# A gated linear attention and two feed-forward layers: the forward products of the gate are made by inverting the backward ones, not by a second scan

## The chip, the cores and the metric

The kernel runs on one core of one Trainium2 chip. The metric is the device time of one execution in microseconds (us). TensorE is the matrix engine (PE in the profile, PEld for its weight loads), VectorE is DVE, ScalarE is ACT, SyncE issues most DMAs (SP).

## The reference, cut to what matters

```python
def _attn_ref(q, k, v, alpha):
    B, H, S, D = q.shape                      # 4, 8, 768, 48
    state = np.zeros((B, H, D, D), dtype=np.float32)
    for t in range(S):
        state = alpha[:, :, t, :, None] * state + np.einsum('bhd,bhe->bhde', k[:, :, t], v[:, :, t])
        y[:, :, t] = np.einsum('bhd,bhde->bhe', q[:, :, t], state)
    return y

x = attention output as rows of 384           # 3072 tokens
g = leaky_relu(x @ w_in, 0.01);  x = g @ w_out     # 384 -> 2048 -> 384
g = elu(x @ w_in2);              out = g @ w_out2  # 384 -> 2048 -> 384
```

`alpha` is between 0.8 and 1.0 and acts per head dimension and token. The attention is made in 24 units of 128 tokens (a chunk of all 8 heads of one batch element).

## The kernel before, in words

For a unit u the host lays out `seqs[u]`: alpha, k and q, all with the head dimension on the partitions (112 rows, two heads with a gap between them) and four groups of 128 tokens along the row. Alpha has one extra column in front of each group (129 columns a group, 517 in all with the last), so that a scan over the whole row starts afresh at each group. One DMA brings all of it into a tile `pack` (three buffers).

`prep_k(u)` (L124 to L135) makes, on VectorE: a scan E from the right over alpha (L129), the product of all later alphas of the chunk; `pe` (L131), the product of the whole chunk, clamped; its reciprocal into the four start columns of the constant tile `d1` (L132); and k times E, in place in `pack` (L134). `prep_F(u)` (L137 to L142) is a second scan F from the left over alpha (L141), which starts at 1/pe and so gives the reciprocal of E at each token. `prep_q(u)` (L144) multiplies q by F in place (L146). Then TensorE makes the scores `sc` of k and q (L160) and transposes k into `pk` (L168); ScalarE copies that into `kn` (L175); VectorE masks the scores into `A` (L182) and decays the state, `T` = S times pe (L189); TensorE makes the output `po` (L214, L220) and the state's update `pu` (L233); VectorE adds up the state S (L257).

The feed-forward layers split each float32 operand into a high and a low part in the format fp32r and use three matmuls for one. For each of 16 slices of 128 hidden units: `hp` (L306), its activation `t` (ScalarE L312, then VectorE's max, L317), the high part `gh` (ScalarE L321), the low part `gl` (VectorE L327), and the sums `y` (L350). There are two buffers of `hp`, and two each of `gh` and `gl`. The weights are converted on the way by `convert_p`, `convert_a`, `convert_b` (L276 to L291).

The order of the work has two parts. The head, units 0 to 7 in the functions `quarter` and the loop behind them (L686 to L783), is fixed: `in_order()` chains the instructions of each engine as they are written. In `quarter(u, 0)` stands `prep_k(u + 1)`, in `quarter(u, 2)` stand `prep_F(u + 1)` and `prep_q(u + 1)`, so unit 8 is prepared there too. From there on (L784 on), where the units 8 to 23 run between the slices of layer 1, a scheduler places the instructions by a model of its own; each engine then works its list in order. Layer 2 follows with no attention in it.

Of the kernel before, what the change touches and what calls it, by code (L numbers as in the profile page):

```python
# [8 lines left out]
F32 = mybir.dt.float32  # L9
# [4 lines left out]
ALU = mybir.AluOpType  # L14
# [5 lines left out]
def attention_two_layers_kernel(  # L20
# [12 lines left out]
    nc = tc.nc  # L33
# [4 lines left out]
    C = CHUNK  # L38
    NU = NT // C
    NC = SEQ // C  # L40
    NP = H // 2
    PD = 2 * D
    PR = 64 + D
    KD = DM // 128
    KF = DFF // 128
    EXT = NP * (C + 1) + 1

    const = ctx.enter_context(tc.tile_pool(name="const", bufs=1))
# [4 lines left out]
    gs_p = ctx.enter_context(tc.tile_pool(name="gs", bufs=2))  # L53
    pack_p = ctx.enter_context(tc.tile_pool(name="pack", bufs=3))
    v_p = ctx.enter_context(tc.tile_pool(name="v", bufs=3))
    pe_p = ctx.enter_context(tc.tile_pool(name="pe", bufs=3))
    at_p = ctx.enter_context(tc.tile_pool(name="at", bufs=1))
    ps_y = ctx.enter_context(tc.tile_pool(name="ps_y", bufs=1, space=PSUM))
    ps_h = ctx.enter_context(tc.tile_pool(name="ps_h", bufs=2, space=PSUM))
# [3 lines left out]
    causal = const.tile([128, C], F32, name="causal")  # L63
    minus = const.tile([PR, PR], F32R, name="minus")
    d0 = const.tile([PR, EXT], F32, name="d0")
    d1 = const.tile([PR, EXT], F32, name="d1")
    bias = const.tile([PR, 2], F32, name="bias")
    outside = const.tile([PR, NU], F32, name="outside")
    far_sum = const.tile([PR, 2], F32, name="far_sum")
# [15 lines left out]
    def constants():  # L85
        make_identity(nc, ident)
        nc.scalar.activation(minus, ident[0:PR, 0:PR], ACTF.Copy, scale=-1.0)
        nc.gpsimd.memset(causal, 1.0)
        nc.gpsimd.affine_select(
            out=causal, in_=causal, compare_op=ALU.is_ge, fill=0.0,  # L90
            base=0, pattern=[[1, C]], channel_multiplier=-1,
        )
        nc.vector.memset(d0, 0.0)
        nc.vector.memset(d0[:, 0:EXT:C + 1], 1.0)
        nc.vector.memset(d1, 0.0)
        nc.vector.memset(bias[:, 0:1], -1.0)
        nc.vector.memset(bias[:, 1:2], -ALPHA_SPAN)
        nc.vector.memset(far_sum[:, 1:2], 1.0)
# [4 lines left out]
    st = {}  # L103
# [17 lines left out]
    def ext(t, off):  # L121
        return t[:, off:off + NP * (C + 1)].rearrange("p (g c) -> p g c", c=C + 1)

    def prep_k(u):  # L124
        t = packs.pop(u)
        kS = t[:, EXT:EXT + NP * C].rearrange("p (g c) -> p g c", c=C)
        qh = t[:, EXT + NP * C:].rearrange("p (g c) -> p g c", c=C)
        E = at_p.tile([PR, EXT], F32, tag="E", name="E")
        nc.vector.tensor_tensor_scan(E[:, ::-1], t[:, EXT - 1::-1], d0[:, ::-1], 0.0, ALU.mult, ALU.add)  # L129
        pe = pe_p.tile([PR, NP, 1], F32, tag="pe", name="pe")  # L130
        nc.vector.tensor_scalar(pe, ext(E, 0)[:, :, 1:2], 1e24, 1e-24, ALU.min, ALU.max)  # L131
        nc.vector.reciprocal(ext(d1, 0)[:, :, 0:1], pe)  # L132
        e2 = E[:, 1:EXT].rearrange("p (g c) -> p g c", c=C + 1)
        nc.vector.tensor_mul(kS, kS, e2[:, :, 1:C + 1])  # L134
        st[u] = dict(kS=kS, qh=qh, pe=pe, pack=t)  # L135

    def prep_F(u):  # L137
        d = st[u]
        t = d["pack"]
        F = at_p.tile([PR, EXT], F32, tag="F", name="F")  # L140
        nc.vector.tensor_tensor_scan(F[:, 0:EXT - 1], t[:, 0:EXT - 1], d1[:, 0:EXT - 1], 0.0, ALU.mult, ALU.add)  # L141
        d["F"] = F  # L142

    def prep_q(u):  # L144
        d = st[u]
        nc.vector.tensor_mul(d["qh"], d["qh"], ext(d.pop("F"), 0)[:, :, 1:C + 1])  # L146

    def attn_prep(u):
        prep_k(u)
        prep_F(u)  # L150
        prep_q(u)
# [352 lines left out]
    def conv_args(layer, kind, m):  # L504
# [10 lines left out]
        else:  # L515
            tags = (("cT", "S"), ("E", "F"))[n]
            tp, ts = [at_p.tile([128, 384], I32, tag=g, name=f"c{g}") for g in tags]
# [152 lines left out]
    with ExitStack():  # L670
        load_unit(0, True)
        constants()
        load_unit(1)
        load_v(0)
# [11 lines left out]
        def quarter(u, i, chain=True):  # L686
            j = unit_block[u]
            xh, xl, _, t = xtile(j)
            off = (u - blocks[j][0]) * C
            if i == 0:  # L690
                attn_pu(u)
                prep_k(u + 1)
                attn_T(u)
            elif i == 1:
                attn_mask(u)
                if chain:
                    attn_pk(u + 1)
                    attn_kn(u + 1)
                attn_po(u)
            elif i == 2:  # L700
                prep_F(u + 1)
                attn_state(u)
                prep_q(u + 1)
                if chain:
                    attn_sc(u + 1)
                attn_xh(u, xh, off)
                attn_rest(u, xh, off)
                load_unit(u + 3)
                load_v(u + 3)
            else:  # L710
                attn_xl_act(u, xl, off)
                st.pop(u)
                if u == blocks[j][0] + blocks[j][1] - 1:
                    gather(t, blocks[j][1] * C)
# [48 lines left out]
        for s, e in enumerate(seq):  # L763
# [3 lines left out]
            if s <= KF:  # L767
                c = 4 if s == 0 else 1 + FIRST + s - 2 - (s - 2) // 4 if s > 1 and s % 4 != 1 else 0
# [33 lines left out]
            if ph == 1 and j == NB - 1:  # L802
                if m == 0:
                    t = x2t[NT // 512 - 1].rearrange("p c f -> p (c f)").bitcast(I32)
# [13 lines left out]
            if ph == 2 and m >= KF - 10 and m % 2 == 0:  # L818
                u = 5 * j + (m - KF + 10) // 2
# [93 lines left out]
```

## Time and profile before

| what | value |
|---|---|
| runs: median (lowest to highest) of 3 | 961.44 us (958.7 to 961.64) |
| the profiled execution: its time, its span | 960.84 us, 959.1 us |
| busy: PE, DVE, ACT | 921.9, 530.0, 449.9 us |
| granted TensorE clock, mean | 0.982 of full speed |

The span is the time from the first to the last instruction, the profiled execution's own time has 1.7 us around it. A digit in the page's slices is the busy share of a fortieth of the span (24 us) in tenths. In the timeline a row is one instruction or a run of like ones, with its start, its duration and, in brackets, how long its engine sat idle before it and what released it. In the chain of waits a piece runs to the start of the next piece, so it can be shorter than the instruction.

### The profile page before, as it was taken

Reading aid. Unit: us, or ns where it says so; the run is one execution under the profiler, and the core shown is the slowest. Engines: PE = TensorE matmul, PEld = TensorE weight load, DVE = VectorE, ACT = ScalarE, POOL = GpSimd, SP = SyncE. Lnnn points to the kernel's source line nnn. Section 1 sums busy time; section 2 is a strip of 40 time slices with the busy share of each in tenths; the row PEclk is TensorE's granted clock in tenths of the full one; section 3 lists DMA queues with packets and bytes.
Section 4 is the critical chain, followed back from the end, with each engine's and each line's share of the span. In section 5 each row is a group of like instructions: output and inputs, shape, how many; then the busy total and the mean of one; then the engine's idle time right before and its main releaser. Section 6 shows DMA issues by size and latency. Waiting matters only on the chain.

```text
span 959.1 us, 13157 instructions
## 1 busy us (share of the span) xinstructions
PE 921.9 (96%) x5242; PEld 777.6 (81%) x5242; DVE 530.0 (55%) x872; ACT 449.9 (47%) x794; POOL 1.1 (0%) x8
## 2 busy tenths in 40 slices
PE   5687999999999999999999999999999999999997
PEld 4565776787888788788888889999999999899996
DVE  6876888855655547454479983433433433333332
ACT  1432765322322322323468894564654744744442
POOL 0000000000000000000000000000000000000000
PEclk9688999999999999999999999999999999999999
DMA  9737343222112121211224420010100200100001
GB/s 229 199 84 206 99 133 98 63 63 58 42 42 74 31 78 43 58 42 51 90 78 131 134 80 10 25 58 1 63 20 1 72 10 1 63 1 1 33 1 37
DMA packets 25092, 62.37 MB, mean 65 GB/s; under 512 B 3936, under 2 KB 7008, under 8 KB 25024
## 3 DMA queue, kind: packets, MB, share of 16 engines
q1 hardware_dynamic: 21360, 48.43, 17.9%
q10 hardware_dynamic: 3664, 13.04, 4.8%
q8 instruction: 43, 0.70, 0.3%
q14 instruction: 25, 0.20, 0.1%
HBM read 54.37 MB, written 4.72 MB: 62 GB/s over the span
## 4 chain that ended last, share of the span: by engine, by line
PE 83%; DVE 6%; DMA 4%; ACT 4%; issue 1%; SPq 1%; DVEq 0%; ACTq 0%
PE hp L381 21%; PE y L350 17%; PE hp L306 17%; PE oa L412 11%; PE o L412 11%; DMA pack<-in_seqs_dram 3%; PE po L214 2%; PE sc L160 2%; PE po L220 2%; DVE x2t L285 1%; DVE x2t L287 1%; DVE E L129 1%; PE pu L233 1%; ACT w L288 1%; ACT x2t L279 1%
## 5 line engine op out<-in xcount | busy, mean ns | idle before, releaser
L306 PE MATMUL hp<-x,w 128*128 128x512 f32 x864 | 219.2, 397 | 7.5 <-DMA x<-x 6.6
L381 PE MATMUL hp<-x,w 128*128 128x512 f32 x864 | 215.4, 393 | 0.0
L306 PEld LDWEIGHTS hp<-x,w 128*128 128x128 f32 x864 | 163.3, 190 | 45.8 <-DMA x<-x 8.1
L381 PEld LDWEIGHTS hp<-x,w 128*128 128x128 f32 x864 | 160.7, 188 | 29.3
L350 PE MATMUL y<-gh,w 128*128 128x512 f32 x576 | 178.2, 398 | 2.1 <-DVE x2t L359 1.1
L390 DVE SCALAR_TENSOR_TENSOR t<-t,hp 128x512 f32<-128x512 f32 x96 | 65.9, 687 | 148.7 <-ACT t L389 148.7
L350 PEld LDWEIGHTS y<-gh,w 128*128 128x128 f32 x576 | 106.1, 189 | 26.1 <-ACT x2t L363 1.3
L312 ACT ACTIVATE t<-hp 128x512 f32<-128x512 f32 x96 | 57.0, 595 | 118.8 <-PE hp L306 118.8
L350 PE MATMUL y<-gl,w 128*128 128x512 f32 x288 | 109.4, 394 | 0.9 <-DVE gl L327 0.9
L321 ACT CAST gh<-t 128x512 fp32r<-128x512 f32 x96 | 59.4, 620 | 102.5 <-PE y L350 55.9
L388 ACT ACTIVATE t<-hp 128x512 f32<-128x512 f32 x96 | 57.3, 597 | 105.7 <-PE hp L381 105.5
L82 DVE TENSOR_TENSOR gl<-t,gh 128x512 fp32r<-128x512 f32 x96 | 66.5, 692 | 70.0 <-ACT gh L79 68.4
L317 DVE TENSOR_TENSOR t<-t,hp 128x512 f32<-128x512 f32 x96 | 65.4, 681 | 69.3 <-ACT t L312 69.1
L412 PE MATMUL oa<-w,gh 128*128 128x384 f32 x384 | 96.7, 337 | 0.0
L412 PE MATMUL o<-w,gh 128*128 128x384 f32 x384 | 94.6, 336 | 0.0
L327 DVE TENSOR_TENSOR gl<-t,gh 128x512 fp32r<-128x512 f32 x96 | 66.1, 689 | 48.7 <-ACT gh L321 46.5
L79 ACT CAST gh<-t 128x512 fp32r<-128x512 f32 x96 | 59.5, 620 | 64.7 <-PE oa L412 34.8
L412 PEld LDWEIGHTS o<-w,gh 128*128 128x128 f32 x384 | 70.6, 188 | 5.4
L412 PEld LDWEIGHTS oa<-w,gh 128*128 128x128 f32 x384 | 70.2, 188 | 2.9
L350 PEld LDWEIGHTS y<-gl,w 128*128 128x128 f32 x288 | 54.3, 189 | 14.3 <-DVE gl L327 2.6
L412 PE MATMUL oa<-w,gl 128*128 128x384 f32 x192 | 63.0, 337 | 0.0
L389 ACT ACTIVATE t<-t 128x512 f32<-128x512 f32 x96 | 60.6, 632 | 2.3
(96 smaller groups left out, 834.9 us busy)
## 6 DMA issues: line engine op xcount, KB each, us to landing
stg<-in_w_dram SPq DMA_DIRECT2D x28, 384.0 KB, 3.1
pack<-in_seqs_dram ACTq DMA_DIRECT2D x13, 674.2 KB, 5.1
x2t<-in_w_dram SPq DMA_DIRECT2D x20, 384.0 KB, 3.5
pack<-in_seqs_dram SPq DMA_DIRECT2D x10, 674.2 KB, 5.4
span<-in_seqs_dram SPq DMA_DIRECT2D x24, 226.2 KB, 2.6
x2t<-in_w_dram SPq DMA_DIRECT2D x32, 144.0 KB, 2.6
out_dram<-osb SPq DMA_DIRECT2D x24, 192.0 KB, 2.0
vt<-in_vals_dram ACTq DMA_DIRECT2D x13, 288.0 KB, 5.2
```

Of the source, the lines that this page charges most:

```text
L79: nc.scalar.copy(dst, src)
L82: (lo_engine or nc.vector).tensor_sub(lo, src, dst.bitcast(F32))
L306: nc.tensor.matmul(hp, lhsT=a[:, kk, :], rhs=x[:, kk, :n], start=(i == 0), stop=(i == 3 * KD - 1))
L317: nc.vector.tensor_max(t, t, hp)
L321: nc.scalar.copy(gh, steps[1, j, m][0])
L327: nc.vector.tensor_sub(gl, t, gh.bitcast(F32))
L350: nc.tensor.matmul(ytiles[j][c], lhsT=a[:, c * 128:(c + 1) * 128], rhs=x, start=(first and i == 0), stop=(last and i == 2),)
L381: nc.tensor.matmul(hp, lhsT=a[:, kk, :], rhs=x[:, kk, :], start=(i == 0), stop=(i == 3 * KD - 1))
L388: nc.scalar.activation(t, hp, ACTF.Relu, scale=-1.0)
L389: nc.scalar.activation(t, t, ACTF.Exp, scale=-1.0)
L390: nc.vector.scalar_tensor_tensor(out=t, in0=t, scalar=-1.0, in1=hp, op0=ALU.add, op1=ALU.max)
L412: nc.tensor.matmul(otiles[j][i], lhsT=a[:, i * 128:(i + 1) * 128], rhs=x, start=(m == 0 and n == 0), stop=(m == KF - 1 and n == 2),)
```

## The change

The second scan is gone. E is kept, its 128 columns a group are inverted in place by one RECIPROCAL instruction on VectorE after k has been multiplied, and q is multiplied by the result. The tile E takes turns between two buffers (those that E and F had). `pe` is no tile of its own any more: `attn_T` reads it from E's first column of each group, which the inversion leaves alone. The clamp is now in the scan (`max` with 1e-24 in place of `add`). The tile `d1`, its memset and the small reciprocal into it are gone.

```diff
-    pe_p = ctx.enter_context(tc.tile_pool(name="pe", bufs=3))
...
-    d1 = const.tile([PR, EXT], F32, name="d1")
...
-        nc.vector.memset(d0, 0.0)
+        nc.vector.memset(d0, 1e-24)
         nc.vector.memset(d0[:, 0:EXT:C + 1], 1.0)
-        nc.vector.memset(d1, 0.0)
...
     def prep_k(u):
         t = packs.pop(u)
-        kS = t[:, EXT:EXT + NP * C].rearrange("p (g c) -> p g c", c=C)
-        qh = t[:, EXT + NP * C:].rearrange("p (g c) -> p g c", c=C)
-        E = at_p.tile([PR, EXT], F32, tag="E", name="E")
-        nc.vector.tensor_tensor_scan(E[:, ::-1], t[:, EXT - 1::-1], d0[:, ::-1], 0.0, ALU.mult, ALU.add)
-        pe = pe_p.tile([PR, NP, 1], F32, tag="pe", name="pe")
-        nc.vector.tensor_scalar(pe, ext(E, 0)[:, :, 1:2], 1e24, 1e-24, ALU.min, ALU.max)
-        nc.vector.reciprocal(ext(d1, 0)[:, :, 0:1], pe)
-        e2 = E[:, 1:EXT].rearrange("p (g c) -> p g c", c=C + 1)
-        nc.vector.tensor_mul(kS, kS, e2[:, :, 1:C + 1])
-        st[u] = dict(kS=kS, qh=qh, pe=pe, pack=t)
+        al, kq = t if isinstance(t, tuple) else (t[:, 0:EXT], t[:, EXT:])
+        kS = kq[:, 0:NP * C].rearrange("p (g c) -> p g c", c=C)
+        qh = kq[:, NP * C:].rearrange("p (g c) -> p g c", c=C)
+        E = at_p.tile([PR, EXT], F32, tag="EF"[u % 2], name="E")
+        nc.vector.tensor_tensor_scan(E[:, ::-1], al[:, ::-1], d0[:, ::-1], 0.0, ALU.mult, ALU.max)
+        e2 = E[:, 1:EXT].rearrange("p (g c) -> p g c", c=C + 1)[:, :, 1:C + 1]
+        nc.vector.tensor_mul(kS, kS, e2)
+        st[u] = dict(kS=kS, qh=qh, pe=ext(E, 0)[:, :, 1:2], e2=e2)
 
     def prep_F(u):
-        d = st[u]
-        t = d["pack"]
-        F = at_p.tile([PR, EXT], F32, tag="F", name="F")
-        nc.vector.tensor_tensor_scan(F[:, 0:EXT - 1], t[:, 0:EXT - 1], d1[:, 0:EXT - 1], 0.0, ALU.mult, ALU.add)
-        d["F"] = F
+        e2 = st[u]["e2"]
+        nc.vector.reciprocal(e2, e2)
 
     def prep_q(u):
         d = st[u]
-        nc.vector.tensor_mul(d["qh"], d["qh"], ext(d.pop("F"), 0)[:, :, 1:C + 1])
+        nc.vector.tensor_mul(d["qh"], d["qh"], d.pop("e2"))
```

The change moves VectorE's list at three kinds of places. (In these lists a scan is written SCALAR_TENSOR_TENSOR, `pack` is k or q of the unit, and a line number of the changed kernel is 2 to 8 lower: L127 is the scan, L129 k times E, L134 the inversion, L138 q times its result.)

VectorE in the head, the preparation of unit 4 in `quarter(3, ...)`, before:

```order
L129 SCALAR_TENSOR_TENSOR E<-pack,d_97 112x517
L131 TENSOR_SCALAR pe<-E 112x4
L132 RECIPROCAL d_98<-pe 112x4
L134 TENSOR_TENSOR pack<-pack,E 112x512
L189 TENSOR_TENSOR T<-S,pe 112x192
L182 TENSOR_TENSOR A<-sc_383,causal 128x512
L182 TENSOR_TENSOR A<-sc_384,causal 128x512
L141 SCALAR_TENSOR_TENSOR F<-pack,d_98 112x516
L257 TENSOR_TENSOR S<-pu,T 112x192
L146 TENSOR_TENSOR pack<-pack,F 112x512
```

and in the change:

```order
L127 SCALAR_TENSOR_TENSOR E<-pack,d_94 112x517
L129 TENSOR_TENSOR pack<-pack,E 112x512
L181 TENSOR_TENSOR T<-S,E 112x192
L174 TENSOR_TENSOR A<-sc_362,causal 128x512
L174 TENSOR_TENSOR A<-sc_363,causal 128x512
L134 RECIPROCAL E<-E 112x4x128
L249 TENSOR_TENSOR S<-pu,T 112x192
L138 TENSOR_TENSOR pack<-pack,E 112x512
```

Nothing else moved in the head: two small instructions are gone between E and k, and the inversion stands where F stood.

VectorE where the fixed order ends, the units 9 and 10, before:

```order
L129 SCALAR_TENSOR_TENSOR E<-pack,d_97 112x517
L131 TENSOR_SCALAR pe<-E 112x4
L134 TENSOR_TENSOR pack<-pack,E 112x512
L132 RECIPROCAL d_98<-pe 112x4
L129 SCALAR_TENSOR_TENSOR E<-pack,d_97 112x517
L141 SCALAR_TENSOR_TENSOR F<-pack,d_98 112x516
L131 TENSOR_SCALAR pe<-E 112x4
L134 TENSOR_TENSOR pack<-pack,E 112x512
L146 TENSOR_TENSOR pack<-pack,F 112x512
L132 RECIPROCAL d_98<-pe 112x4
L317 TENSOR_TENSOR t<-t,hp 128x512
L141 SCALAR_TENSOR_TENSOR F<-pack,d_98 112x516
```

and in the change (x2 is two in a row):

```order
L127 SCALAR_TENSOR_TENSOR E<-pack,d_94 112x517 x2
L129 TENSOR_TENSOR pack<-pack,E 112x512 x2
L134 RECIPROCAL E<-E 112x4x128 x2
L309 TENSOR_TENSOR t<-t,hp 128x512 x2
L138 TENSOR_TENSOR pack<-pack,E 112x512
L249 TENSOR_TENSOR S<-pu,T 112x192
L234 TENSOR_TENSOR x<-po,x 112x4x128
L138 TENSOR_TENSOR pack<-pack,E 112x512
L319 TENSOR_TENSOR gl<-t,gh 128x512 x2
```

Both inversions now stand ahead of the first max of `t` (L309); before, one F stood ahead of it and one behind it.

VectorE in the part that the scheduler orders, unit 12, before:

```order
L129 SCALAR_TENSOR_TENSOR E<-pack,d_97 112x517
L317 TENSOR_TENSOR t<-t,hp 128x512
L131 TENSOR_SCALAR pe<-E 112x4
L134 TENSOR_TENSOR pack<-pack,E 112x512
L132 RECIPROCAL d_98<-pe 112x4
L141 SCALAR_TENSOR_TENSOR F<-pack,d_98 112x516
L327 TENSOR_TENSOR gl<-t,gh 128x512
```

and in the change:

```order
L127 SCALAR_TENSOR_TENSOR E<-pack,d_94 112x517
L129 TENSOR_TENSOR pack<-pack,E 112x512
L134 RECIPROCAL E<-E 112x4x128
L309 TENSOR_TENSOR t<-t,hp 128x512
L174 TENSOR_TENSOR A<-sc_1625,causal 128x512
L174 TENSOR_TENSOR A<-sc_1626,causal 128x512
L138 TENSOR_TENSOR pack<-pack,E 112x512
L319 TENSOR_TENSOR gl<-t,gh 128x512
```

The max of `t` now stands behind the inversion; before, it stood right behind E.

## Rows read from the trace of the kernel before

**Rows 1.** The page: busy time of PE, busy tenths of PE and DVE, TensorE's waits at L350.

```profile
PE 921.9 (96%) x5242; PEld 777.6 (81%) x5242; DVE 530.0 (55%) x872; ACT 449.9 (47%) x794; POOL 1.1 (0%) x8
...
PE   5687999999999999999999999999999999999997
...
DVE  6876888855655547454479983433433433333332
...
L350 PE MATMUL y<-gh,w 128*128 128x512 f32 x576 | 178.2, 398 | 2.1 <-DVE x2t L359 1.1
```

**Rows 2.** Groups of DVE instructions: line, operation, tiles, shapes, count | busy us, mean ns.

```profile
L129 DVE TENSOR_TENSOR_SCAN E<-pack,d 112x517 f32<-112x517 f32 x24 | 29.6, 1233 | 24.7 <-DMA pack<-in_seqs_dram 24.7
L141 DVE TENSOR_TENSOR_SCAN F<-pack,d 112x516 f32<-112x516 f32 x24 | 29.4, 1225 | 0.1
L146 DVE TENSOR_TENSOR pack<-pack,F 112x512 f32<-112x512 f32 x24 | 16.5, 689 | 0.4
...
L291 DVE TENSOR_TENSOR w<-x2t,w 128x768 fp32r<-128x768 f32 x16 | 15.3, 958 | 5.1 <-ACT w L288 5.0
...
L284 DVE TENSOR_SCALAR x2t<-x2t 128x768 int32<-128x768 int32 x16 | 8.9, 554 | 0.0
...
L132 DVE RECIPROCAL d<-pe 112x4 f32<-112x4 f32 x24 | 4.2, 176 | 0.3
L131 DVE TENSOR_SCALAR pe<-E 112x4 f32<-112x4 f32 x24 | 4.1, 169 | 0.8
```

**Rows 3.** The instructions on the tile pe: durations in ns, least/median/most.

```profile
L131 DVE TENSOR_SCALAR pe<-E x24: 146/170/172, 5.8 to 422.3; 112x4 f32<-112x4 f32 x24
```

**Rows 4.** Timeline, 0 to 60 us: start us, us, engine, line, what [idle before <-releaser].

```profile
9.97 1.23 DVE L129 TENSOR_TENSOR_SCAN E<-pack,d 112x517 f32<-112x517 f32 x1 [1.31 <-DMA pack<-in_seqs_dram]
...
14.70 0.68 DVE L146 TENSOR_TENSOR pack<-pack,F 112x512 f32<-112x512 f32 x1
...
16.73 2.08 PE L160 MATMUL sc<-pack 48*128 48x128 f32 x16
...
23.45 1.23 DVE L129 TENSOR_TENSOR_SCAN E<-pack,d 112x517 f32<-112x517 f32 x1 [1.33 <-DMA pack<-in_seqs_dram]
...
38.53 0.68 DVE L146 TENSOR_TENSOR pack<-pack,F 112x512 f32<-112x512 f32 x1
```

**Rows 5.** The chain of waits, 0 to 60 us: start us, us, engine, tile, line.

```profile
25.10 0.58 DVE pack L134
...
27.14 1.14 DVE F L141
...
41.47 2.01 PE sc L160 x16
```

**Rows 6.** The chain of waits, 60 to 100 us.

```profile
68.77 1.15 DVE F L141
...
70.64 1.15 DVE E L129
```

**Rows 7.** Timeline, 60 to 100 us, the end of unit 7's preparation.

```profile
77.81 0.68 DVE L146 TENSOR_TENSOR pack<-pack,F 112x512 f32<-112x512 f32 x1
...
79.89 1.16 PE L160 MATMUL sc<-pack 48*128 48x128 f32 x16
```

**Rows 8.** Timeline, 164 to 182 us, DVE alone: units 9 to 11.

```profile
164.91 1.23 DVE L129 TENSOR_TENSOR_SCAN E<-pack,d 112x517 f32<-112x517 f32 x1
...
170.59 0.66 DVE L317 TENSOR_TENSOR t<-t,hp 128x512 f32<-128x512 f32 x1
...
173.48 0.69 DVE L327 TENSOR_TENSOR gl<-t,gh 128x512 fp32r<-128x512 f32 x1
...
180.29 1.26 DVE L359 TENSOR_TENSOR x2t<-y,x2t 128x512 f32<-128x512 f32 x2
```

**Rows 9.** Timeline, 193 to 204 us: unit 12.

```profile
194.38 1.24 DVE L129 TENSOR_TENSOR_SCAN E<-pack,d 112x517 f32<-112x517 f32 x1 [2.89 <-DMA pack<-in_seqs_dram]
195.53 0.66 DVE L317 TENSOR_TENSOR t<-t,hp 128x512 f32<-128x512 f32 x1
...
200.04 2.21 PE L306 MATMUL hp<-x,w 128*128 128x512 f32 x9
```

## The prediction

> **What bounds the kernel now.** I read the page first. TensorE is busy for 921.9 of 959.1 us, and its row of slices is full from the fifth of the forty on; the gaps lie in the first four, up to 96 us, and there VectorE is at 6 to 8 tenths [rows 1]. So VectorE sets the pace at most in the head. Behind it TensorE waits for next to nothing that VectorE does; the longest is one 1.1 us wait for the additions to `x2t` (L359), where the fixed order ends [rows 1]. The chain of waits says where VectorE counts in the head: k times E of unit 3 and F of unit 3 lie on it [rows 5], F of unit 6 and E of unit 7 too [rows 6]; F of units 4, 5, 7 and 8 does not. The timeline gives the margins: VectorE idled 1.31 us before E of unit 1 and 1.33 us before E of unit 3, both times for the load of `pack` [rows 4].
>
> **What goes.** Each unit loses F, 1.225 us [rows 2]; on the chain F holds VectorE for 1.14 us, since the next instruction starts 0.09 us before F's end [rows 5]. Between E and k times E the clamp (0.169 us) and the small reciprocal (0.176 us) go [rows 2]: unit 3's E starts at 23.45 [rows 4], k times E at 25.10 [rows 5], 1.65 us later, of which the scan itself is 1.23. So 0.4 us goes there. The memset of `d1` ran before the first load arrived and is worth nothing. The scan with `max` in place of `add` I take to cost the same; it still does one multiplication and one other operation per element.
>
> **What comes.** One RECIPROCAL of 112x512 per unit, called R here. The trace has that instruction only on 112x4, at 176 ns [rows 2], so its price must be worked out. Instructions on two tensors take 689 ns for 512 elements and 958 for 768 [rows 2]: 269 ns for 256 more, 1.05 ns an element, and so 689 - 538 = 151 ns of fixed cost. If RECIPROCAL has the same fixed cost, its four elements took 176 - 151 = 25 ns, 6.25 ns each, and R takes 151 + 512 x 6.25 = 3350 ns.
>
> The bounds. Below: the clamp, also on four elements, takes 169 ns though its elements should cost 4 [rows 2], so most of RECIPROCAL's extra 25 ns may be a fixed cost of short instructions. R is then an ordinary instruction of 0.69 us, or, at the rate of the fastest one-tensor instruction (768 elements in 554 ns, [rows 2]), 151 + 512 x 0.52 = 0.42 us. Above: the clamp's shortest case, 146 ns [rows 3], leaves 142 ns of fixed cost, hence (176 - 142)/4 = 8.5 ns an element and R = 142 + 4352, about 4.5 us. I take 3.35: the rows of the same instruction and the fixed cost that fits every long instruction give it, and 0.69 needs a reason why an instruction with one operand takes longer than the clamp, which does two operations. But four elements are a short lever, so both ends stay in the range.
>
> The Trainium skill (VectorE: DVE Perf Modes, section First, the fixed hardware budget) says that the reciprocal is an iterative divide with a repeat count of 8. If that is eight cycles an element, R is an estimated 4.3 us of stream and the sum would be the third rival's. No row has the long case.
>
> **The sum.** R holds VectorE for 3.35 - 0.09 = 3.26 us, so it costs 3.26 - 1.14 = 2.12 us more than F where nothing hides it.
>
> Units 0 to 2, start: before E of unit 1, 2.12 - 0.4 less the idle 1.31 is +0.4. Unit 1: its q is ready 0.4 - 0.4 + 2.12 = 2.1 us later; before, q ended at 15.38 and its scores began at 16.73 [rows 4], a margin of 1.35, so the scores are 0.8 late. Unit 2's masks wait for them, its R adds 2.12, and the idle 1.33 before E of unit 3 goes: 0.8 + 2.1 - 1.3 = **+1.6** at 23.45.
>
> Units 3 to 5: -0.4 between E and k of unit 3, +2.12 at F (27.14, [rows 5]), -0.4 in unit 4: **+1.3**. Unit 4's R is hidden: q ended at 39.21 [rows 4], its scores began at 41.47 [rows 5], a margin of 2.26 against 2.12. Without that margin it would cost all 2.12. Unit 5's R falls into VectorE's wait for the gather of x and costs nothing.
>
> Units 6 and 7: -0.4, +2.12 at F (68.77), -0.4 at E of unit 7 (70.64) [rows 6]: **+1.3**. Unit 7's q ended at 78.49 and its scores began at 79.89 [rows 7]: 2.12 - 1.40 is **+0.7**. The head is +4.9 us. Unit 8's R stands before a long wait for the next gather.
>
> Units 9 and 10: the list has E twice, k twice, R twice, then the max of `t`. From 164.91 [rows 8] that is 2 x 1.15 + 2 x 0.60 + 2 x 3.26, so the max starts at 174.9, not at 170.59 [rows 8]: +4.3. Next late are `gh` and `gl` (173.48), and the additions to `x2t` (180.29, [rows 8]), which have a third R ahead of them. TensorE had no margin for these (the 1.1 us wait). I take **+4.5**; if TensorE's list has other slices to work on meanwhile it may be half.
>
> Units 11 to 23, 13 of them among full TensorE work: in unit 12 the max stands behind R. It ends at 194.38 + 1.27 + 0.60 + 3.26 + 0.66 = 200.17; its buffer is needed by `hp` at 200.04 [rows 9]. So the margin that is there now (195.53 + 0.66 to 200.04, 3.85 us) is just used up, and behind it TensorE waits. I take 0.1 us a unit, **+1.1** in all; with margins as in unit 12 it is between 0 and 2.
>
> The sum: 960.84 (the profiled execution's own time) + 4.9 + 4.5 + 1.1 = 971.3, so **971 us**. The median of the runs is 0.6 us above that execution, less than I can resolve. VectorE's busy time goes from 530 to 530 + 24 x 3.35 - 29.4 - 4.2 - 4.1 = 573 us.
>
> With 5.0 ns an element (the clamp's excess taken off a third) R is 2.7 us and the same steps give +4.5; with 7.25, 3.9 us and +17. The forecast's own range is 965 to 978.
>
> **The rivals.**
>
> First, *R runs at an ordinary instruction's rate*, 0.69 us, 0.60 of it on the chain: faster. For it: the clamp's unexplained 14 ns. Against: RECIPROCAL is still 7 ns above the clamp [rows 2]. The start gains nothing, since E of unit 3 waits for its load; units 3 and 4, and again 6 and 7, gain 0.4 + 0.54 + 0.4 = 1.34 each, units 9 to 11 at most TensorE's wait of 1.1. That is 960.84 - 2.7 - 1.1 = 957.0, or 956.5 with R at 0.42. It decides below some 2.2 ns an element. The Trainium skill (Vector Engine (DVE) Microarchitecture Reference, section 5.2 Measured stream behaviour on trn2) has a rule of this kind: built-in one-source operations take 1.04 ns a column and a fixed cost. By that rule the time would be this 957; the long rows here agree with its rate (1.05 ns), the scans (1233 ns for 517 elements) do not. Chance 0.27.
>
> Second, *no change*: between 2.2 and 3.6 ns an element (R of 1.3 to 2.0 us) the 0.8 us saved around k pays for R in the head and the rest hides in idle time; at units 9 and 10 up to 1.7 us is lost. 960 to 963. For it: that rate lies between the two readings of one row. Chance 0.16.
>
> Third, *R at 8.5 ns, 4.5 us*: +3.26 a unit. The same steps give +12.8 in the head (unit 4 then is late by 1.0 and unit 7 by 1.9), +6.8 at units 9 to 11, and now the max in the later units passes the time at which `hp` needs its buffer by 1.3 us; over half of 13 units some +6. 986 us, TensorE no longer full between 190 and 430 us. For it: only the shortest clamp as fixed cost. Chance 0.15.
>
> That the change doesn't do what it says, for example that the second buffer of E brings a new wait, I find no place for: `pe` of a unit is read before the scan two units later writes that buffer, on the same engine.
>
> **How the numbers follow.** Forecast 0.42, no change 0.16, faster 0.27, worst 0.15. A change below 0.3% (2.9 us) can't be told from none. Of the first rival 0.22 is faster by more and 0.05 is not; of the second 0.12 stays within and 0.04 is slower; the forecast and the third are slower. So faster 0.22, same 0.17, slower 0.61. The range 956 to 984 leaves out most of the third rival (0.12), the low edge of the first (0.05) and a little for what I have not seen.
>
> **What would show it.** The mean of the RECIPROCAL group with 24 instructions decides first: 2.7 to 3.9 us for the forecast, 0.4 to 0.7 for the first rival, 4.4 and above for the third. Then E of unit 3 at about 25 us, E of unit 7 at about 75, the max behind units 9 and 10 about 9 us later than before (4.9 of it from the head), and TensorE's slices still full from 190 us on. Wrong would be a fast R with no gain (the head is then held by loads and gathers alone), or a slow R with no loss (the margins are larger than I read).

## The result and the profile after

The changed kernel takes **974.38 us** (median of 4 runs, 974.19 to 974.48); the kernel before, run beside it, 960.54 us (4 runs, 958.7 to 961.64). The ratio is 1.0135, with a 95% interval of 1.0108 to 1.0163: slower by 13 us. The prediction was 971 us, with a range of 956 to 984.

The page of the changed kernel, to be held against [rows 1]: busy times, and the slices of PE and DVE.

```profile
PE 925.5 (95%) x5242; PEld 778.8 (80%) x5242; DVE 574.2 (59%) x823; ACT 450.2 (46%) x794; POOL 1.1 (0%) x8
...
PE   4678999899999999999999999999999999999997
...
DVE  8889688976767666655469993433433333433332
```

Its groups of DVE instructions, the inversion and the scan.

```profile
L134 DVE RECIPROCAL E<-E 112x512 f32<-112x512 f32 x24 | 80.3, 3349 | 0.4
L127 DVE TENSOR_TENSOR_SCAN E<-pack,d 112x517 f32<-112x517 f32 x24 | 29.5, 1231 | 20.2 <-DMA pack<-in_seqs_dram 20.2
```

VectorE gained the 44 us of busy time that was counted (573 predicted, 574.2 here). The inversion takes 3349 ns, and the scan with `max` what it took with `add` [rows 2]. VectorE is busy only 59% of the span, so the 13 us lie in a few places. The timeline finds them: its DVE rows at the starts of E.

```profile
25.61 1.23 DVE L127 TENSOR_TENSOR_SCAN E<-pack,d 112x517 f32<-112x517 f32 x1
...
52.45 1.23 DVE L127 TENSOR_TENSOR_SCAN E<-pack,d 112x517 f32<-112x517 f32 x1
...
68.45 1.23 DVE L127 TENSOR_TENSOR_SCAN E<-pack,d 112x517 f32<-112x517 f32 x1
71.79 3.35 DVE L134 RECIPROCAL E<-E 112x512 f32<-112x512 f32 x1
75.78 1.23 DVE L127 TENSOR_TENSOR_SCAN E<-pack,d 112x517 f32<-112x517 f32 x1
...
172.34 2.35 DVE L127 TENSOR_TENSOR_SCAN E<-pack,d 112x517 f32<-112x517 f32 x2
...
175.80 6.56 DVE L134 RECIPROCAL E<-E 112x512 f32<-112x512 f32 x2
182.27 1.22 DVE L309 TENSOR_TENSOR t<-t,hp 128x512 f32<-128x512 f32 x2
```

The same places in the kernel before, as far as no group of rows above has them, and the issue of the second gather of x before and after (SPq is SyncE's queue):

```profile
47.60 1.23 DVE L129 TENSOR_TENSOR_SCAN E<-pack,d 112x517 f32<-112x517 f32 x1
...
65.08 1.23 DVE L129 TENSOR_TENSOR_SCAN E<-pack,d 112x517 f32<-112x517 f32 x1
...
86.33 3.79 SPq L271 DMA_DIRECT2D x<-x  x6
```

```profile
94.10 3.79 SPq L263 DMA_DIRECT2D x<-x  x6
```

| place | before | after | later by |
|---|---|---|---|
| E of unit 3 | 23.45 [rows 4] | 25.61 | 2.2 |
| E of unit 5 | 47.60 | 52.45 | 4.9 |
| E of unit 6 | 65.08 | 68.45 | 3.4 |
| issue of the second gather | 86.33 | 94.10 | 7.8 |
| E of unit 9 | 164.91 [rows 8] | 172.34 | 7.4 |
| first max of `t` behind it | 170.59 [rows 8] | 182.27 | 11.7 |
| span | 959.1 | 972.5 | 13.4 |

So 3.4 us are lost up to unit 6, 4.0 more up to unit 9, and 6.0 from there on, nearly all of it at units 9 and 10. The way to unit 6 isn't even: E of unit 5 is 4.9 late, and 1.5 of that comes back before E of unit 6.

### The profile page after: what moved, and what is told of

It reads as the page before. It is cut to its first block, busy times and chain, and to the rows that moved or that the text cites. A ratio compares the mean times of both kernels' runs of the same rounds, so it can differ in the third digit from the quotient of the medians.

```text
span 972.5 us, 13122 instructions
## 1 busy us (share of the span) xinstructions
PE 925.5 (95%) x5242; PEld 778.8 (80%) x5242; DVE 574.2 (59%) x823; ACT 450.2 (46%) x794; POOL 1.1 (0%) x8
## 4 chain that ended last, share of the span: by engine, by line
PE 83%; DVE 8%; ACT 4%; DMA 2%; issue 1%; SPq 1%; DVEq 0%; ACTq 0%
PE hp L373 21%; PE hp L298 17%; PE y L342 17%; PE oa L404 10%; PE o L404 10%; DVE E L134 2%; PE sc L152 2%; PE po L206 2%; PE po L212 2%; DVE x2t L279 1%; DVE x2t L277 1%; PE pu L225 1%; ACT x2t L271 1%; DVE E L127 1%; ACT x2t L272 1%
## 5 line engine op out<-in xcount | busy, mean ns | idle before, releaser
L309 DVE TENSOR_TENSOR t<-t,hp 128x512 f32<-128x512 f32 x96 | 65.0, 679 | 48.1 <-ACT t L304 48.0
L134 DVE RECIPROCAL E<-E 112x512 f32<-112x512 f32 x24 | 80.3, 3349 | 0.4
```

The lines of the kernel that those rows point to most:

```text
L134: nc.vector.reciprocal(e2, e2)
L309: nc.vector.tensor_max(t, t, hp)
```

## Where the time went in units 6 and 7, and in 9 and 10

TensorE's rows around the scores of unit 6 in the timeline of the kernel before (the state's part of unit 5's `po`, unit 6's scores, `pu` and first part of `po`); then the same of the changed kernel, with the transposes ahead of them.

```profile
69.83 1.08 PE L220 MATMUL po<-pack,T 48*48 48x128 f32 x16
70.84 1.16 PE L160 MATMUL sc<-pack 48*128 48x128 f32 x16
...
73.43 0.67 PE L233 MATMUL pu<-vt,kn 128*64 128x48 f32 x16 [1.02 <-DVE A L182]
...
74.56 1.09 PE L214 MATMUL po<-A,vt 128*64 128x128 f32 x16
```

```profile
71.33 0.60 PE L160 MATMUL pk<-ident,pack 112*128 112x112 f32 x4 [2.03 <-DVE A L174]
...
73.47 1.95 PE L212 MATMUL po<-pack,T 48*48 48x128 f32 x16
76.01 2.08 PE L152 MATMUL sc<-pack 48*128 48x128 f32 x16 [0.59 <-DVE pack L138]
...
78.84 1.09 PE L225 MATMUL pu<-vt,kn 128*64 128x48 f32 x16
...
80.79 1.93 PE L206 MATMUL po<-A,vt 128*64 128x128 f32 x16
```

The same instructions take nearly twice as long: the four groups in both lists 7.05 us in place of 4.00. Only 0.59 us is a wait for q, which the inversion makes later. The table of windows gives the granted clock (the third number from the end): here 72 to 83 us, before and after.

```profile
72.00:83.00 11.00, 9.69 (x100) 7.50 (x101) 10.36 (x18) 4.90 (x8) 0.00 (x0) 1.00 0.98 243
```

```profile
72.00:83.00 11.00, 10.36 (x87) 8.13 (x87) 9.38 (x10) 3.75 (x7) 0.00 (x0) 0.53 0.62 147
```

It was full before and is near half now: 1.2 GHz in place of 2.4, behind an idle stretch of 2.03 us. That the inversion brings this fall about is not shown by these rows; kernels without any inversion here lose the same time (below, under Neither inversion nor idle).

At units 9 and 10 there are a wait and a lower clock too: TensorE's waits from 165 to 200 us, its timeline row, with a row of `hp` in the kernel before, and the stretch behind the wait.

```profile
PE hp L298 <- DVE t L309: 3.3, 1, 3.3
```

```profile
182.96 6.89 PE L298 MATMUL hp<-x,w 128*128 128x512 f32 x18 [3.28 <-DVE t L309]
```

```profile
172.08 2.20 PE L306 MATMUL hp<-x,w 128*128 128x512 f32 x9
```

```profile
182.00:190.00 8.00, 7.04 (x20) 5.59 (x21) 6.87 (x12) 1.94 (x4) 0.00 (x0) 0.60 0.04 11
```

This is the one wait in that stretch, and the max behind both inversions ends it. The clock is 0.60 behind it: 18 matmuls of `hp` take 6.89 us; before, nine took 2.20. The kernel before had a wait of its own here, 1.1 us for `x2t` [rows 1], so the waits add 2.2 us and the slower work 2.5: 4.7 of the 6.0 us. The other 1.3 is not traced; TensorE's list is in another order here, too (18 matmuls of `hp` in a row). From 200 us to layer 2 TensorE waits for nothing, before and after.

## The experiments

Times stand beside runs of the kernel before on the same chip (medians 960.1 to 960.7 us); ratios carry their 95% interval.

**The length of the inversion, four elements and half.** The same instruction at the same place, on 4 and on 256 of the 512 elements.

```diff
-        nc.vector.reciprocal(e2, e2)
+        nc.vector.reciprocal(e2[:, :, 0:1], e2[:, :, 0:1])     # short_r
+        nc.vector.reciprocal(e2[:, :, 0:64], e2[:, :, 0:64])   # half_r
```

> The changed kernel with RECIPROCAL on one token of each group only (112x4 instead of 112x512): the inversion of the other 127 tokens is left out, all else of the change stays (scan with max, two buffers of E, pe read from E, no small chain). If the length of the inversion is the whole loss, 956 to 959 us: the gain of the removed scan in the head, 1.3 us at two places, and up to 1.1 us at units 9 to 11, against 960.5. If the rest of the change (buffers, the new order) costs something by itself, 961 or more.

> The changed kernel with RECIPROCAL on 64 of the 128 tokens of each group (112x256): half of the inversion is left out. At 6.25 ns an element and 151 ns fixed the instruction takes 1.75 us, 0.5 us more than the scan F that it stands for, while 0.4 us is saved around k. By the sums of the prediction: 959 to 962 us, no change that can be told. If the loss follows the instruction's length in a straight line between 957 and 974, 965 us.

Measured: 957.23 us, ratio 0.9969 (0.995 to 0.9987), and 963.1 us, ratio 1.0031 (1.0015 to 1.0047). Without the inversion's length the rest of the change gains 3 us, so the whole loss comes with that length. Half of it already costs 3 us: more than my sums gave (959 to 962) and less than the straight line (965), so neither expectation was met. The groups of the two kernels:

```profile
L134 DVE RECIPROCAL E<-E 112x4 f32<-112x4 f32 x24 | 4.2, 176 | 0.3
```

```profile
L134 DVE RECIPROCAL E<-E 112x256 f32<-112x256 f32 x24 | 41.9, 1747 | 0.3
```

With 3349 for 512 elements, three lengths lie on one line: (3349 - 1747) / 256 = 6.26 ns an element and 145 to 151 ns fixed.

**Which units pay.** A second scan, in place on alpha, for some units, and the inversion for the rest (E's two buffers, the clamp in the scan and the missing `pe` stay).

```diff
+        if scanned(u):      # late_only: u <= 8, head_only: u > 8, scan_9_10: u in (9, 10), lean: all
+            nc.vector.tensor_tensor_scan(F[:, 0:EXT - 1], F[:, 0:EXT - 1], d1[:, 0:EXT - 1], 0.0, ALU.mult, ALU.add)
+        else:
             nc.vector.reciprocal(d["e2"], d["e2"])
```

> Inversion for the units 9 to 23, second scan (as in the run with the second scan kept) for the units 0 to 8. VectorE's list at units 9 and 10 is that of the change. If the loss has two places, head (7.5 us in the two traces) and units 9 and 10 (6 us, of which 3.3 us is TensorE's wait for the max of t and 2.8 us its lower granted clock behind it), this takes 964.5 to 966 us. If the lower clock would come back anyway, or if the delay of the head made units 9 and 10 late, 961 to 963.

> Inversion for the units 0 to 8, second scan (in place on alpha) for the units 9 to 23. If the head loses 7.5 us by itself, 967 to 968.5 us, with TensorE full and at the higher granted clock from about 108 us on. If part of the head's delay is made up by the weight conversions that follow it, 963 to 966.

> The changed kernel with the second scan for the units 9 and 10 only; all others invert. If the later units (11 to 23) lose nothing, as TensorE's missing waits there say, this equals the run with the inversion in the head alone: 967 to 968.5 us. If the later units' margins are used up, as the prediction's 1.1 us has it, 969 to 971.

> The second scan is kept (in place on alpha, from the small reciprocal), with the parts of the change that take work away: the clamp is in the first scan, pe is read from E, and the small reciprocal stands behind k times E. The output is the reference's. Per unit 0.17 us of clamp goes and the small reciprocal is off the way to k. If VectorE's path in the head is what counts, 0.3 to 0.4 us at four places: 958.5 to 959.5 us. If the loads and gathers alone hold the head, 960.5.

| kernel | inversions in units | us | ratio (95%) |
|---|---|---|---|
| late_only | 9 to 23 | 965.45 | 1.0068 (1.0043 to 1.0093) |
| head_only | 0 to 8 | 968.21 | 1.0076 (1.0052 to 1.0101) |
| scan_9_10 | all but 9 and 10 | 968.47 | 1.0084 (1.0058 to 1.0109) |
| lean | none | 960.89 | 1.0005 (0.9987 to 1.0023) |

Head and rest add up: 0.76% and 0.68% are 1.44%, and the whole change is 1.35%. The 13 units from 11 on cost nothing that can be measured: scan_9_10 inverts in all of them and takes what head_only takes. In late_only the max of `t` holds TensorE up just as in the changed kernel, but the clock stays full behind it (1.00 from 176 to 190 us), and the same 18 matmuls take 4.38 us, not 6.89:

```profile
175.98 4.38 PE L310 MATMUL hp<-x,w 128*128 128x512 f32 x18 [3.29 <-DVE t L321]
```

From E of unit 9 (165.37) to the end it takes 3.3 us more than the kernel before, the changed kernel 6.0. So the wait comes with the inversions of units 9 and 10 in both; the lower clock behind it came in the profiled execution of the one kernel and not in that of the other. My expectation for lean was wrong: it was at E of unit 8 in 77.37 us, 1.0 ahead of the kernel before, but at E of unit 9 in 166.35, 1.4 behind it.

**Twice the inversion**, to see how much room the later units have (the second one inverts back).

```diff
         nc.vector.reciprocal(e2, e2)
+        nc.vector.reciprocal(e2, e2)
```

> The changed kernel with RECIPROCAL twice in a row on the same tile (the second undoes the first, so q is multiplied by E itself): 3.26 us more per unit on VectorE. The head's margins are gone, so the head loses about 3.3 us at nearly each unit from 1 to 7: +20 to +25 against the change. Units 11 to 23 tell whether their margin (3.85 us in unit 12 before) is real: if so, TensorE waits there for at most 1 us a unit and the time is 995 to 1010 us; if the margin was already used up, over 2 us a unit and 1020 us or more.

Measured: 1004.42 us, ratio 1.0457 (1.0431 to 1.0482). All TensorE waits from 215 to 520 us, in which each unit's inversions hold VectorE for 6.7 us:

```profile
PE y L343 <- DVE gl L320: 1.1, 1, 1.1
PE sc L153 <- DVE pack L139: 0.2, 1, 0.2
```

The room in the later units is real and wide. E of unit 9 starts at 199.84, so 27.5 of the 30 us that this run is above the changed kernel lie in the head.

**One inversion less, in unit 6 or in unit 7.** The edit is that of the table, with `u == 6` and `u == 7`.

> The changed kernel with the second scan (in place on alpha, 1.2 us in place of the 3.35 us inversion) in unit 6 alone; all other units invert. Read by the start of E of unit 9, which is 172.34 us in the changed kernel. By the prediction's steps unit 6's inversion stands on the path for its full 2.1 us less 0.4, so E of unit 9 at 170.2. By the reading of the changed kernel's chain its cost is larger, since behind it the scores of unit 6 took 2.10 us at a lower granted clock: E of unit 9 at 169.0 to 169.7. Time 971 to 972.5.

> The second scan in unit 7 alone, all other units invert. The prediction charged unit 7's inversion 0.7 us (2.12 less a margin of 1.40 in front of its scores): then E of unit 9 at 171.6. The rival, from the changed kernel's chain: E, k, T and the mask stand behind the inversion in VectorE's own list, so it costs its full 2.1 us: E of unit 9 at 170.2. Time 972 to 973.5.

Measured: 974.41 and 974.17 us (one run each), E of unit 9 at 172.41 and 172.23. Both expectations failed, the prediction's and its rival's: nothing comes through to E of unit 9. The issue of the gather and the `hp` behind it, in the timelines of scan_6 and of scan_7:

```profile
75.41 2.08 PE L164 MATMUL sc<-pack 48*128 48x128 f32 x16
...
93.52 3.80 SPq L275 DMA_DIRECT2D x<-x  x6
...
98.89 3.65 PE L310 MATMUL hp<-x,w 128*128 128x512 f32 x7 [3.96 <-DMA x<-x]
```

```profile
93.40 3.89 SPq L275 DMA_DIRECT2D x<-x  x6
...
98.86 3.36 PE L310 MATMUL hp<-x,w 128*128 128x512 f32 x7 [4.05 <-DMA x<-x]
```

Either one gains only 0.6 to 0.7 us at the gather (94.10 with both). In scan_6 the scores no longer wait for q, but still take 2.08 us: the clock had fallen before them. And in all three kernels `hp` starts at 98.9 us, however early the gather was issued; why it lands no sooner these runs don't settle.

**Work in the idle stretch ahead of the fall.** The second slice's `hp` is made twice, in place, where TensorE idled 2.03 us.

```diff
-        for a, x in ((wh, xh), (wl, xh), (wh, xl)):
+        for a, x in ((wh, xh), (wl, xh), (wh, xl)) * times:
...
-                pe_h(n)
+                ffn1_h(n[1], n[2], 2 if s == 0 else 1)
```

> The changed kernel, with the nine matmuls of the second slice's hp made twice in the same place (the second time over the first's result, so the output is the reference's). It adds 2.2 us of TensorE work just where TensorE idled 2.03 us (69.3 to 71.3 us) before the granted clock fell to half for 72 to 83 us; nothing else is moved. Theory: units 6 and 7 lost their time through that clock and not through the inversions' places, since either inversion taken out alone gained only 0.6 to 0.7 us at the gather. Then the clock stays up in 72 to 83 us, the issue of the gather moves from 94.1 us to about 91 and E of unit 9 from 172.3 to 169 to 171; time 971 to 973. Rival: the clock falls for another reason, or the inversions alone set the pace there: then nothing moves, or everything behind 70 us is 0.2 us later, and the time is 974 to 975.

Measured: 975.26 us, ratio 1.0155 (1.0138 to 1.0172): the theory failed, and the rival's time is nearest. The rows show what happened; first `hp` and the scores, then the clock of the stretch that had been at half and of the one behind it.

```profile
67.93 4.24 PE L298 MATMUL hp<-x,w 128*128 128x512 f32 x18
...
76.85 1.61 PE L152 MATMUL sc<-pack 48*128 48x128 f32 x16 [1.98 <-DVE pack L138]
```

```profile
70.00:77.00 7.00, 5.02 (x48) 3.72 (x48) 6.93 (x8) 2.82 (x5) 0.00 (x0) 1.00 0.17 34
77.00:85.00 8.00, 7.93 (x59) 6.17 (x60) 6.77 (x8) 3.24 (x5) 0.00 (x0) 0.57 1.03 272
```

With the clock up, TensorE is through sooner and then waits 1.98 us for unit 6's q, which the inversion holds, and the fall comes there. As long as the inversion stands in unit 6, filling one pause only moves the pause and the fall.

**Neither inversion nor idle.** Lean, with the same repetition and with matmuls that fill two more idle stretches.

```diff
+        for r in range(fill):      # 48 ahead of the first hp, 12 ahead of the hp behind the second gather
+            if j == 0:
+                d, p = st[UB], r % NP
+                nc.tensor.matmul(hp[:, 0:C], lhsT=d["kS"][0:D, p, :], rhs=d["qh"][0:D, p, :], start=True, stop=True)
+            else:
+                nc.tensor.matmul(hp, lhsT=wh[:, r % KD, :], rhs=xt[0][0][:, r % KD, :n], start=True, stop=True)
```

> The kernel with the second scan kept in place (the one that ran 960.89 us), with TensorE given work in three idle stretches of the head, all else the same: 48 matmuls of k and q ahead of the first hp (4.47 us idle, then nine matmuls in 4.65 us), the second slice's hp made twice (2.08 us idle, then half clock for 66 to 77 us), 12 matmuls of x ahead of the hp behind the second gather (3.85 us idle, then 4.73 us for nine). All write into hp ahead of its real nine, so the output is the reference's. Theory: with no inversion in the way and no idle stretch in front, the clock stays up, units 6 and 7 pass in 3 to 4 us less, each of the two hp takes 2.2 to 2.5 us; E of unit 9 comes at 160 to 163 us in place of 166.35, and the time is 955 to 958, below both kernels. Rival: what is gained ahead of 100 us is lost again behind other waits (gathers, weights, the conversions of 100 to 165 us), or the idle time only moves: 959.5 to 962.

Measured: 971.39 us, ratio 1.0108 (1.0079 to 1.0137): a miss. The rows of the fill, then of units 6 and 7 and of the `hp` behind the gather:

```profile
43.28 20.85 PE L311 MATMUL hp<-pack 48*128 48x128 f32 x96
...
83.20 1.16 PE L164 MATMUL sc<-pack 48*128 48x128 f32 x16
...
98.51 3.79 SPq L275 DMA_DIRECT2D x<-x  x6
...
103.42 2.87 PE L316 MATMUL hp<-x,w 128*128 128x512 f32 x9 [0.75 <-DMA x<-x]
```

My fill was far too long: 20.85 us for a gap of 4.47. I had sized it by the scores' 72 ns a row at full clock, but 48 of these matmuls leave 96 rows, the clock stayed at half, and a row takes 217 ns where the scores' take 130 (2.08 / 16). So E of unit 6 is 15.4 us later than in lean, and the total tells nothing about the idea. What the run does show is the part behind it, measured from its own E of unit 6 (77.62) to the issue of the gather:

| kernel | inversions in units 6 and 7 | scores of unit 6 at | E of unit 6 to the gather, us | E of unit 6 to E of unit 9, us |
|---|---|---|---|---|
| before | no | full clock | 21.25 | 99.83 |
| lean_warm | no | full clock | 20.89 | 98.15 |
| lean | no | half | 24.62 | 104.13 |
| late_only | no | half | 24.61 | 104.69 |
| short_r | on four elements | half | 24.62 | 103.91 |
| half_r | on half of the elements | full, half clock only behind them | 22.74 | 101.56 |
| changed | yes | half | 25.65 | 103.89 |
| warm | yes | falls during them | 25.19 | 103.77 |

The rows of lean that this rests on:

```profile
62.22 1.23 DVE L132 TENSOR_TENSOR_SCAN E<-pack,d 112x517 f32<-112x517 f32 x1
...
166.35 2.35 DVE L132 TENSOR_TENSOR_SCAN E<-pack,d 112x517 f32<-112x517 f32 x2
```

```profile
68.72 2.08 PE L164 MATMUL sc<-pack 48*128 48x128 f32 x16
```

With the scores at half clock and no inversion the stretch up to the gather takes 3.4 us more than before (24.62 against 21.25); the two inversions add 1.0 to that, and at E of unit 9 nothing is left of the 1.0. So the 4 us that the changed kernel loses between E of unit 6 and E of unit 9 go with the lower clock and not with the inversions of units 6 and 7: lean, late_only and short_r, which have no full inversion there, take as long. Against lean, all that the inversions cost in the head stands at E of unit 6 already: 68.45 against 62.22 there, 172.34 against 166.35 at E of unit 9. Why the clock falls in these kernels and not in the kernel before stays open. From E of unit 6 to E of unit 9 lean_warm takes 6 us less than lean. That a shorter fill would bring lean to about 955 us is an estimate from these two; it was not run.

**The inversion on ScalarE**, as exp(-ln E), to free VectorE.

```diff
-        nc.vector.reciprocal(e2, e2)
+        nc.scalar.activation(e2, e2, ACTF.Ln)
+        nc.scalar.activation(e2, e2, ACTF.Exp, scale=-1.0)
```

> The inversion is moved off VectorE: ScalarE makes exp(-ln E) in place, two ACTIVATE instructions of 112x512 per unit, some 0.6 to 0.7 us each by the other ScalarE rows, and a table load of up to 1.3 us (the one row of it in the kernel before) ahead of each if the two functions and the others of ScalarE don't share a table. Theory that only VectorE's holding time of 3.35 us costs anything: then 957 to 959 us, as with the inversion of four elements (957.2). Rival, that the length of the step itself counts, because q, the scores and the masks wait for it: 1.4 us of work and up to 3.8 us of loads per unit stand in the same place as the inversion's 3.35, so 965 to 980, and ScalarE's other work at units 8 to 23 is late by the loads as well.

Measured: 994.83 us, ratio 1.036 (1.0342 to 1.0378): the rival, and more. ScalarE's groups, and TensorE's longest waits:

```profile
L134 ACT ACT_TABLE_LOAD x23 | 29.5, 1283 | 2.6 <-DVE pack L129 2.3
L135 ACT ACT_TABLE_LOAD x23 | 29.5, 1283 | 0.4
L134 ACT ACTIVATE E<-E 112x512 f32<-112x512 f32 x24 | 15.2, 633 | 11.2 <-DVE pack L129 10.9
```

```profile
PE sc L153 <- DVE pack L139: 27.3, 7, 10.0
```

Nearly every inversion needs two table loads: 2 x 1283 + 2 x 633 = 3.8 us, longer than the 3.35 on VectorE, in the same place ahead of q; the scores wait 27.3 us for q (13.2 in the changed kernel). VectorE falls to 498.9 us of busy time and the kernel is 35 us slower: that VectorE is free gains nothing while q comes later. The run does not separate the lateness of q from the delay of ScalarE's other work behind the loads. Nor was it tried with fewer loads; the two ACTIVATEs alone are 1.27 us, about as long as the scan F. The Trainium skill (ScalarE: Activation LUTs, section What ACT_TABLE_LOAD costs) gives 1283 ns for such a load, as measured here.

No kernel here beats both clearly; lean equals the kernel before, and the 957 us belong to a kernel that leaves the inversion out.

## Why the prediction was right, and where its sum was off

**The price of the inversion** was right: 3350 ns from a row on four elements, 3349 measured, on a line that half the length confirms. That decided among the rivals: an ordinary rate (957), 2.2 to 3.6 ns an element (no change) and 8.5 ns (986) all fell with it. The Trainium skill (VectorE: DVE Perf Modes, section First, the fixed hardware budget) speaks of a repeat count of 8; 6.26 ns is nearer to six steps of the 1.05 ns that an element takes elsewhere, and the measurement decides.

**Units 0 to 5** came out nearly right: +1.6 and +1.3 predicted, 2.9 in all; 2.2 and 1.2 measured. For units 3 to 5 that is partly luck, since two errors cancel. Unit 4's inversion was to be hidden by the margin ahead of its scores, so that E of unit 5 would be 2.9 late; but E of unit 5 stands behind that inversion in VectorE's own list, and it was 4.9 late. Then 1.5 came back, which the sum did not have: the output `po` of unit 5 ran at the lower clock before and at the full one now.

```profile
53.89 1.97 PE L214 MATMUL po<-A,vt 128*64 128x128 f32 x16
```

```profile
58.49 1.15 PE L206 MATMUL po<-A,vt 128*64 128x128 f32 x16
```

**Units 6 and 7** are the step that failed: "-0.4, +2.12 at F (68.77), -0.4 at E of unit 7", +1.3, and unit 7's +0.7. The sum charged 2.0 us to the two inversions and held the clock constant. Taken out one at a time they returned 0.6 and 0.7 at the gather and nothing at E of unit 9. The stretch from E of unit 6 to the gather lost 4.4 us, not 2.0, because TensorE's clock fell to half there, and kernels without these inversions lose 3.4 of that and the same 4 us up to E of unit 9. So the head cost 7.4 at E of unit 9 (4.9 predicted), with the right sign but by another mechanism. Which idle stretch lets the clock fall is not settled: 1.90 us of idle at 66 us in the kernel before was not followed by a fall, 2.03 us here was.

**Units 9 and 10**: the max was to be 4.3 us later from E of unit 9 on, and is (9.93 us behind it, 5.68 before). The wait was as forecast; the price of 4.5 was too low: TensorE waited 3.3 us, 2.2 more than before, and then lost 2.5 at a lower clock, which the sum did not have; 6.0 in all, of which 1.3 is not traced. In late_only the clock did not fall there.

**Units 11 to 23** were charged 1.1 us and cost nothing. The wait "just used up" in unit 12 never came, and even a doubled inversion leaves 1.3 us of waits there: one margin was read as if all 13 units shared it.

The sum was 4.9 + 4.5 + 1.1 = 10.5 over the 960.84 of the profiled execution; measured 7.4 + 6.0 + 0 = 13.4. Of what was to show it, E of units 3 and 7 came at 25.61 and 75.78 (25 and 75), and TensorE's slices stayed full; the max came 11.7 us later, not 9.

## What to carry to other kernels

A long instruction in place of a short one costs its extra length only where the step stands ahead of something that waits; find these places by the margins on the chain, since the same 2.1 us cost nothing in 13 of 24 units. Where TensorE waits, read the granted clock behind the wait too: here the slower work cost about as much as the waits themselves. And before a loss is put down to the change, look for it in a kernel without the change: the 4 us at units 6 and 7 stand in lean as well. Take a price from two lengths of the same instruction where the trace has them; one short row was enough here only because the fixed cost was known from others.

## What the runs showed of the hardware that was not expected

- RECIPROCAL takes 6.26 ns an element on VectorE, six times what a multiplication takes, and is linear from 4 to 512 elements.
- 96 rows of matmuls of 48 x 128, back to back, kept TensorE busy for all of 43 to 64 us, and the granted clock stayed at half. This is that stretch in lean_warm:

```profile
43.00:64.00 21.00, 21.00 (x102) 20.74 (x98) 8.14 (x12) 1.66 (x3) 0.00 (x0) 0.50 0.26 63
```

- Behind a wait of 3.28 us in the changed kernel the granted clock was at half (0.60 from 182 to 190 us), behind the same wait of 3.29 us in late_only it was full (1.00 from 176 to 190).
- At that half clock the fill's matmuls took 217 ns a row, the scores of the same shape 130. The scores alternate between two halves of the rows (`r = slice(64 * j, 64 * j + D)`), the fill used one. The Trainium skill (TensorE: Matmul & The Clock Gate, section Why this matters for your kernels) says that matmuls on distinct groups of rows run side by side, which would explain it; no run here separates it from the fill's one target in the accumulator.
